# A planned attention-and-FFN kernel: new load sum, modelled instruction fetches, tanh in pairs and a split every fourth unit

## The chip, the cores and the metric

The kernel runs on one core of a Trainium2 chip. The metric is device time in microseconds; before the change it is 1190.25 us, the median of three runs from 1188.72 to 1191.48. Engines are written as in the profile: PE is TensorE, DVE is VectorE, ACT is ScalarE, POOL is GpSimd, SP is SyncE, whose queue issues all DMAs.

## The reference

For an input of 2048 tokens with 512 features the output is the sum of three things: the input, multi-head attention of its layer norm, and a gated FFN. Attention has 32 heads of only 16 features.

```
xn = _layernorm(x, axis=-1)
return x + _A_ref(xn, A_wqkv, A_wo) + _B_ref(xn, B_w1, B_w3, B_w2)
# _A_ref: q, k, v of xn @ wqkv, 32 heads of 16
scores = jnp.einsum("bhqd,bhkd->bhqk", q, k) * (Dh ** -0.5)
p = _softmax(scores, axis=-1)
o = jnp.einsum("bhqk,bhkd->bhqd", p, v)         # then o @ wo
# _B_ref: gate = x @ w1, up = x @ w3, F = 1792
h = _silu(gate) * up                            # then h @ w2
```

Scores for 32 heads, 2048 queries and 2048 keys are computed twice: once to find each query's maximum, once transposed for the exponentials.

## The kernel before

**Units.** Four heads share a tile of 128 partitions, 32 rows a head: 16 features, then two extra rows that carry the negative maximum in two parts of bf16, and rows that do not matter. A unit is four heads by 256 queries (128 at the start and in the last 16 units). There are 73 units, numbered 0 to 72.

**Pass 1, the maxima.** For each unit TensorE computes scores with queries on the partitions, two matmuls of 512 keys at a time (line 1164), and VectorE takes the maximum of these 1024 columns (line 1203). POOL joins the partial maxima, and a DMA transpose (line 1351) with two DMAs (line 1347) puts the negative maxima into the extra rows of the query tile QT.

**A split.** In some units, one of the 1024-column maxima is taken in part on ScalarE: TensorE forms a difference of two score blocks, ScalarE its relu (line 1271, into RB), and VectorE joins it with other scores in one combined instruction (line 1192). The dictionary SPLIT lists the units: from SPLIT_LO = 20 to 12 before the last, every SPLIT_STEP.

**Pass 2, the exponentials.** TensorE computes the scores transposed, keys on the partitions, with the maximum already subtracted, and ScalarE takes the exponential of a block of 512 columns (line 1477) or of two blocks in neighbouring PSUM banks (line 1507). A block is scored with 32 rows of the array by default (line 1452, "row"). It can also be scored over all 128 rows ("wide", lines 667 and 671, operand BD): BD holds a head's query rows with zeros in the other heads' rows, and four DMAs per unit, in bd_prep, copy 32 partitions each into it. PV (line 671, operand Vaug) multiplies the exponentials by the values and a column of ones; its result goes to U, is divided by way of small DMAs (Lc, rd, R) and lands in the tile for the output projection.

**The FFN** runs beside this in 56 chunks of 128 hidden features by 512 tokens. ffn_pair makes a gate tile (zg, line 966) and an up tile (ub, line 970); the tanh of zg (th, line 960) is put on lazyq, from which ScalarE takes work when it has a gap; POOL then makes t, a and hT with three instructions. zg, th and ub have two buffers, chosen by the chunk's parity.

**The order is planned.** The program builds one instruction list for each engine with a simulated clock. At each step every engine offers its next piece of work with an estimated start (pick_dve, pick_act, pick_pe, pick_pool, pick_sp), and the earliest is emitted. P.op, P.pe and P.dma estimate when an instruction starts and when its result can be seen. What has been emitted gets semaphore waits afterwards, in emit_engine; on the chip every engine runs its list in this order. Rules such as leads and limits are in RULES; for every 24 steps of the two passes TUNE names one entry of SETS that overrides some of them.

**The load sum.** _heat gives each TensorE instruction a weight, and heat(st) is the weighted sum over the last 2 us (RECENT). Under HEAT_FILL = 1.5 the planner may place a spare matmul (fill_cand: the identity times xnT, its result is never read). Under HEAT_WIDE = 0.9 it scores a block wide; under HEAT_P1 = 1.2 it may issue a pass-1 pair more than once; FFN tiles are held back above HEAT_TILE.

Of the kernel before, what the change touches and what calls it, by code (L numbers as in the profile page):

```python
# [7 lines left out]
ACTF = mybir.ActivationFunctionType  # L8
# [20 lines left out]
class _Item:  # L29
    __slots__ = ("fn", "reads", "writes", "occ", "lat", "cb", "pred", "name", "exp", "busy")  # L30

    def __init__(self, fn, reads, writes, occ, lat=None, cb=None, pred=None, name="", exp=None, busy=0.1):
        self.busy = busy
        self.fn = fn
# [10 lines left out]
class _Prog:  # L45
# [3 lines left out]
    def __init__(self):  # L49
# [12 lines left out]
        self.act_end = 0.0  # L62

# [82 lines left out]
    def pe(self, fn, reads, writes, mode, groups, dur, name="", first=None):  # L146
# [32 lines left out]
    def dma(self, fn, reads=(), writes=(), name="", eng="sp", lat=2.3, occ=0.62, busy=0.1):  # L179
# [11 lines left out]
        op.vis = start + lat + over  # L191
        self.ndma += 1
# [66 lines left out]
def _c_mm(n):  # L259
    return n / 2400.0 + (0.007 if n >= 512 else 0.004)  # L260
# [6 lines left out]
def _build(nc, A_x, A_wqkv, A_wo, B_w1, B_w3, B_w2, out):  # L267
# [28 lines left out]
    AUG_LAT = 3.0  # L296
# [25 lines left out]
    SPLIT_STEP = 5  # L322
# [7 lines left out]
        dict(ROW_LEAD=0.55),  # L330
# [3 lines left out]
        dict(A_LEAD=0.69),  # L334
        dict(TOL=0.05),
        dict(TOL=0.15),
        dict(PAIR_WAIT=0.1),
        dict(PV_LEFT=2),
        dict(RELAX=0.05),
# [3 lines left out]
        dict(HEAT_FILL=1.15),  # L343
        dict(HEAT_FILL=2.0),
        dict(HEAT_FILL=3.0),
        dict(HEAT_WIDE=1.15),
        dict(HEAT_WIDE=1.4),
        dict(HEAT_P1=1.5),
        dict(HEAT_TILE=1.3),
        dict(HEAT_TILE=1.6),  # L350
        dict(PAIR_WAIT=0.1, HEAT_FILL=2.0),
        dict(ROW_LEAD=0.55, WIDE_LEAD=0.45, BD_NEAR=0.1),
        dict(BD_NEAR=0.5, MIN_PIECE=2, TOL=0.15, HEAT_FORCE=1.0),
        dict(PV_LEFT=8, HEAT_WIDE=1.4, TOL=0.05, LAZY_GAP=0.02),
        dict(ROW_LEAD=0.4, TOL=0.05, MATE=0.0, HEAT_WIDE=0.0),
        dict(TEN_MID=2, PAIR_TEN=2, TOL=0.05),
        dict(MIN_PIECE=2, MATE=0.0, ROW_LEAD=0.5),
        dict(A_LEAD=0.6, HEAT_FORCE=1.0, WIDE_LEAD=0.7),
        dict(HEAT_FORCE=1.0, PAIR_WAIT=0.1, ROW_LEAD=0.43),
# [1765 lines left out]
```

## Time and profile before

| what | value |
| --- | --- |
| median of 3 runs | 1190.25 us |
| the profiled execution's own time | 1188.72 us |
| its span | 1187.0 us |
| granted TensorE clock, mean | 0.999 |
| PE busy | 1136.2 us, 96% |
| DVE busy | 1170.7 us, 99% |
| ACT busy | 1165.9 us, 98% |
| POOL busy | 459.4 us, 39% |
| DMA packets | 144068, 56.28 MB |

The span runs from the first to the last instruction; the execution's time is 1.7 us longer. A row of a group shows line, engine, operation, output and inputs, shapes and count, then busy time in us and mean ns of one, then the engine's idle time before it. A row of a timeline shows the start and the time from the first start to the last end in us, and how many equal instructions follow one another (x60). On VectorE and ScalarE an instruction starts before the one before it has ended, so the distance of two starts is the price of one, not its length. Idle times under 150 ns are not listed. Sums over groups hide this overlap; a wait is put down to the work that ended it.

### The profile page before, as it was taken

What the parts mean: (1) busy time and instruction counts of PE and PEld (TensorE: products, weight loads), DVE (VectorE), ACT (ScalarE), POOL (GpSimd) and SP (SyncE); (2) the same over time, 40 slices, a digit from 0 to 9 for tenths busy, and PEclk for the clock granted to TensorE, in tenths of its full rate; (3) what the DMA queues carried; (4) which work ended last, traced back from release to release, by engine and by line L of the source; (5) the groups of instructions that cost most, each with busy time, mean ns of one, the idle gap of its engine ahead of it and who ended that gap; (6) DMA issues with size and microseconds to landing.
All of it is one profiled execution on the core that took longest, in us unless ns stands there. A gap on an engine that the chain in (4) does not pass through costs nothing.

```text
span 1187.0 us, 35168 instructions
## 1 busy us (share of the span) xinstructions
PE 1136.2 (96%) x14555; PEld 518.3 (44%) x14555; DVE 1170.7 (99%) x1083; ACT 1165.9 (98%) x2216; POOL 459.4 (39%) x921
## 2 busy tenths in 40 slices
PE   8999999999999999999999999999999999999998
PEld 4443444433444444443444434443434443445554
DVE  8999999999999999999999999999999999999996
ACT  8899999999999999999999999999999999999998
POOL 6245454333423236344332245434332246233320
PEclk9999999999999999999999999999999999999999
DMA  7223231211111122111111122111110121111110
GB/s 244 65 61 97 73 89 41 61 27 42 38 29 40 37 62 49 36 42 31 40 33 27 40 67 50 32 41 33 39 34 23 40 67 23 28 26 23 22 21 22
DMA packets 144068, 56.28 MB, mean 47 GB/s; under 512 B 106028, under 2 KB 143908, under 8 KB 143908
## 3 DMA queue, kind: packets, MB, share of 16 engines
q1 hardware_dynamic: 143908, 54.02, 18.0%
q8 instruction: 115, 1.88, 0.7%
q14 instruction: 45, 0.37, 0.1%
HBM read 38.67 MB, written 6.74 MB: 38 GB/s over the span
## 4 chain that ended last, share of the span: by engine, by line
ACT 49%; PE 25%; DVE 21%; DMA 2%; issue 1%; POOL 1%; SPq 0%; ACTq 0%; POOLq 0%
ACT PT L1477 34%; DVE part L1203 21%; PE ps L667 10%; ACT PT L1507 9%; PE ps L671 5%; PE ps L1452 5%; PE ps L1164 4%; ACT zg L966 1%; ACT ub L970 1%; ACT th L960 1%; ACT U L1571 1%; PE ps L1813 1%; DMA rd<-Rc 1%; DMA BD<-QT 1%; ACT kq L855 1%
## 5 line engine op out<-in xcount | busy, mean ns | idle before, releaser
L1203 DVE TENSOR_REDUCE part<-ps 128x2 f32<-128x1024 f32 x1008 | 1143.1, 1216 | 2.5 <-PE ps L1452 1.6
L1477 ACT ACTIVATE PT<-ps 128x512 bf16<-128x512 f32 x1642 | 881.4, 691 | 4.6 <-PE ps L1452 1.8
L1452 PE MATMUL ps<-QT,KT 32*128 32x256 bf16 (+1 forms) x3520 | 456.3, 257 | 7.1 <-DMA QT<-Zs 0.4
L1164 PE MATMUL ps<-KT,QT 32*128 32x512 bf16 x2074 | 420.6, 383 | 5.4 <-DVE part L1203 2.9
L1452 PEld LDWEIGHTS ps<-QT,KT 32*128 32x128 bf16 x3520 | 162.4, 92 | 160.6 <-ACT PT L1477 72.2
L1507 ACT ACTIVATE PT<-ps 128x1024 bf16<-128x1024 f32 x203 | 219.9, 1117 | 0.0
L671 PE MATMUL ps<-PT,Vaug 128*17 128x256 bf16 (+1 forms) x4672 | 191.9, 261 | 4.7 <-ACT PT L1507 2.4
L1596 POOL TENSOR_TENSOR Rc<-Lc,mone 128x8 f32<-128x8 f32 (+1 forms) x69 | 105.0, 1522 | 225.1 <-DMA Lc<-U 224.8
L1164 PEld LDWEIGHTS ps<-KT,QT 32*128 32x128 bf16 x2074 | 104.2, 91 | 157.9 <-DVE part L1203 79.0
L667 PE MATMUL ps<-xnT,w 128*128 128x512 bf16 (+3 forms) x639 | 159.6, 320 | 5.3 <-ACT PT L1507 1.0
L667 PE MATMUL ps<-BD,KT 128*128 128x256 bf16 (+1 forms) x786 | 136.6, 266 | 5.4 <-ACT PT L1507 2.8
L671 PEld LDWEIGHTS ps<-PT,Vaug 128*17 128x17 bf16 x4672 | 89.7, 90 | 79.2 <-issue 52.9
L667 PE MATMUL ps<-xnT,ident 128*128 128x512 bf16 (+3 forms) x309 | 89.2, 335 | 12.3 <-DVE part L1203 4.5
L667 PEld LDWEIGHTS ps<-xnT,w 128*128 128x128 bf16 x639 | 49.8, 97 | 78.2 <-issue 39.0
L1328 POOL TENSOR_TENSOR mx<-part 128x16 f32<-128x16 f32 (+1 forms) x67 | 14.2, 212 | 180.2 <-DVE part L1203 180.0
L667 PEld LDWEIGHTS ps<-BD,KT 128*128 128x128 bf16 x786 | 62.3, 98 | 42.5 <-ACT PT L1477 9.5
L667 PE MATMUL ps<-w,hT 128*128 128x512 bf16 (+3 forms) x342 | 77.7, 309 | 0.0
L945 POOL TENSOR_SCALAR t<-th 128x512 f32<-128x512 bf16 x56 | 34.8, 622 | 104.8 <-ACT th L960 104.0
L949 POOL TENSOR_TENSOR hT<-a,t 128x512 bf16<-128x512 f32 x56 | 71.0, 1268 | 2.8
L671 PE MATMUL ps<-BD,KT 128*32 128x256 bf16 (+1 forms) x1464 | 68.4, 268 | 0.3 <-DMA BD<-QT 0.2
L947 POOL TENSOR_TENSOR a<-zg,ub 128x512 f32<-128x512 bf16 x56 | 64.6, 1154 | 9.5 <-ACT ub L970 9.5
L1616 POOL TENSOR_TENSOR wk_on<-U,R 128x256 bf16<-128x256 f32 (+1 forms) x36 | 23.0, 638 | 72.4 <-DMA R<-rd 72.4
(110 smaller groups left out, 710.4 us busy)
## 6 DMA issues: line engine op xcount, KB each, us to landing
w<-in_B_w_dram SPq DMA_DIRECT2D x112, 128.0 KB
R<-rd SPq DMA_DIRECT2D x55, 128.0 KB
QT<-qd SPq DMA_DIRECT2D x31, 128.0 KB
KT<-kd SPq DMA_DIRECT2D x28, 128.0 KB
BD<-QT SPq DMA_DIRECT2D x220, 16.0 KB
xr<-in_A_x_dram SPq DMA_DIRECT2D x16, 128.0 KB
out_dram<-osb SPq DMA_DIRECT2D x16, 128.0 KB
qd<-kq SPq DMA_DIRECT2D x15, 128.0 KB
```

Source lines behind the costliest of these rows:

```text
L667: return e.matmul(bank(bk)[:, c0 + a:c0 + b], make_lhsT(0, 128), rhs_ap(0)[:, a:b], start=start, stop=stop, **kw)
L671: ins = e.matmul(bank(bk)[32 * i:32 * i + m, c0 + a:c0 + b], make_lhsT(i), rhs if (a, b) == (0, ncols) else rhs[:, a:b], start=start, stop ...
L945: q.append(_Item(lambda e: e.tensor_scalar(t1[:, :], th[:, ss, :], 1.0, 1.0, ALU.mult, ALU.add), [("th", ss)], [("t1",)], 0.62, 0.72))
L947: q.append(_Item(lambda e: e.tensor_tensor(a32[:, :], zg[:, ss, :], ub[:, ss, :], ALU.mult), [("zg", ss), ("ub", ss)], [("a32",)], 1.1, 1.25))
L949: q.append(_Item(lambda e: e.tensor_tensor(hT[:, hslot(idx), :], a32[:, :], t1[:, :], ALU.mult), [("a32",), ("t1",)], [("hT", hslot(idx))] ...
L1164: ins = e.matmul(bank(2 * sl + i), QT[32 * j:32 * j + 32, qs, q * 128:(q + 1) * 128], KT[32 * j:32 * j + 32, g, c_ * 512:(c_ + 1) * 512], ...
L1203: redq.append(_Item(lambda e: e.tensor_reduce(dst, pair_ap.rearrange("p (a b) -> p a b", b=512), AX.X, ALU.max), writes, [("part", par, qt ...
L1452: ins = e.matmul(bank(b)[:, i * nq:(i + 1) * nq], KT[32 * j:32 * j + 32, g, (k0 + i) * 128:(k0 + i + 1) * 128], QT[32 * j:32 * j + 32, qs, ...
L1477: expq.append(_Item(lambda e: e.activation(PT[:, sl, :], bank(b), ACTF.Exp, scale=SCALE), [("ps", b)], [("PT", sl)], _c_act(512), cb=cb, e ...
L1507: return _Item(lambda e: e.activation(PT[:, s0:s1 + 1:s1 - s0, :], ps8[:, b0:b1 + 1:b1 - b0, :], ACTF.Exp, scale=SCALE), [("ps", b0), ("ps ...
L1596: poolq["nrm"].append(_Item(lambda e: e.tensor_tensor(Rc[:, pp, 0:nl], Lc[:, pp, 0:nl], mone[:, 0:nl], ALU.pow), [("Lc", pp), ("mone",)], ...
L1616: poolq["nrm"].append(_Item(lambda e: e.tensor_tensor(onorm[ob][:, g, q0:q0 + nq], U[:, us, 0:nq], R[:, pp, 0:nq], ALU.mult), [("U", us)] ...
```

## The change

Some of it alters what is emitted:

- Tanh is taken for two chunks together: one instruction of 128x1024 after the second chunk's gate, for chunks of even and odd number. POOL's work for the first chunk can start only then.
- SPLIT_STEP goes from 5 to 4.
- The copies into BD carry 21 partitions for 32. The rows that are left out stay zero from the start; the 16 features and the two extra rows are among the 21.

The rest alters the planner's estimates and rules, and so the order:

- _heat has new weights for every kind of matmul (the limits in RULES stay).
- P.pe counts TensorE's instructions and notes when it is expected to fetch the next 256 (_FETCH); P.dma makes a transfer that is not marked narrow land later if it coincides with a fetch.
- Expected latencies of several small transfers are lowered (AUG_LAT 3.0 to 2.55; the two extra rows 2.0 to 1.75; BD 2.1 to 2.0; R 3.7 to 3.5).
- SETS and TUNE are replaced.

```diff
+_FETCH = (180, 256, 2.0255, 25.5, 1.0, 2.05, 0.7, 0.15)
 def _heat(name, mode, groups, full, dur):
     if mode == "row":
-        return (0.846 if name.startswith("p2") else 0.713) * len(groups)
-    n = 1 if full else 8 if name.startswith("w2") else 4
-    return (1.23 if name.startswith("PV") else 2.32) + 0.0284 * n / dur
+        return (1.04 if name.startswith("p2") else 0.447) * len(groups)
+    if name.startswith("PV"):
+        return 2.16
+    if not full:
+        return 3.6
+    return 3.0 if name.startswith("w2") else 2.75
...
+        self.pe_n += _FETCH[2] * (mm or getattr(fn, "mm", 1))
+        if self.pe_n >= self.fetch_at:
+            self.fetch.append(start + _FETCH[4])
+            self.fetch_at += _FETCH[1]
...
+        if not narrow and self.heat:
+            soon = self.heat[-1][0] + (self.fetch_at - self.pe_n) / _FETCH[3] + _FETCH[4]
+            for t in self.fetch[-2:] + [soon]:
+                if start + _FETCH[6] - _FETCH[5] / 2 < t < op.vis - _FETCH[7]:
+                    op.vis = max(op.vis, t + _FETCH[5])
...
-    AUG_LAT = 3.0
+    AUG_LAT = 2.55
...
-    SPLIT_STEP = 5
+    SPLIT_STEP = 4
...
+            pair_done[idx] = part_done
+
             def zg_done(op):
-                lazyq.append(_Item(lambda e: e.activation(th[:, ss, :], zg[:, ss, :], ACTF.Tanh),
-                                   [("zg", ss)], [("th", ss)], 0.52, cb=part_done))
-                lazy_t[0] = P.free["act"]
+                if ss == 1:
+                    lazyq.append(_Item(lambda e: e.activation(th[:, :, :], zg[:, :, :], ACTF.Tanh),
+                                       [("zg", 0), ("zg", 1)], [("th", 0), ("th", 1)], 0.947,
+                                       cb=lambda op: [pair_done[i](op) for i in (idx - 1, idx)]))
+                    lazy_t[0] = P.free["act"]
                 part_done(op)
...
-                later_dma(lambda e, j=j: e.dma_start(BD[32 * j:32 * j + 32, u % 2, j, 0:nq],
-                                                     QT[32 * j:32 * j + 32, qs, q0:q0 + nq]),
+                later_dma(lambda e, j=j: e.dma_start(BD[32 * j:32 * j + 21, u % 2, j, 0:nq],
+                                                     QT[32 * j:32 * j + 21, qs, q0:q0 + nq]),
```

SETS goes from 55 to 52 entries, and TUNE's 128 numbers all refer to the new list.

More of the change, by code (lines that the diff above doesn't have):

```diff
@@ L144, in pe_start, with pe @@
         return t
-    def pe(self, fn, reads, writes, mode, groups, dur, name="", first=None):
+    def pe(self, fn, reads, writes, mode, groups, dur, name="", first=None, mm=0):
         op = _Op()
@@ L675, in part @@
                 f.full = full
+                f.mm = 1 if full else n
                 return f
@@ L1167, in f @@
                     return ins
-                P.pe(f, reads, writes, "row", rows, again * _c_mm(512) * (3 - len(rows)), name="p1_%d" % n, first="dve")
+                P.pe(f, reads, writes, "row", rows, again * _c_mm(512) * (3 - len(rows)), name="p1_%d" % n, first="dve",
+                     mm=again * len(cells))
                 p1_n[0] += 1
```

101 lines of the change are left out of this document (53 added, 48 removed), and 12 rows, old and new, of the table TUNE.

## The prediction

> **What bounds the kernel now.** I read the head of the page first, then the stages, then VectorE's and ScalarE's instructions in order of time, and last the chain.
>
> ```profile
> PE 1136.2 (96%) x14555; PEld 518.3 (44%) x14555; DVE 1170.7 (99%) x1083; ACT 1165.9 (98%) x2216; POOL 459.4 (39%) x921
> ACT 49%; PE 25%; DVE 21%; DMA 2%; issue 1%; POOL 1%; SPq 0%; ACTq 0%; POOLq 0%
> 58.00:1029.00 971.00, 937.26 (x11211) 407.97 (x11210) 970.80 (x866) 968.19 (x1838) 387.81 (x725) 1.00 0.18 45
> 1029.00:1168.00 139.00, 132.32 (x2523) 74.86 (x2522) 136.79 (x124) 136.01 (x264) 43.17 (x132) 1.00 0.10 21
> 1168.00:1187.00 19.00, 13.21 (x366) 7.83 (x362) 8.65 (x26) 13.97 (x19) 0.00 (x0) 0.95 0.09 30
> ```
>
> In the stage rows the columns are the stage, its length, then busy time of PE, weight loads, DVE, ACT and POOL, the granted clock, and the DMA share. Through the body VectorE (970.80 of 971) and ScalarE (968.19) are both full, so the page does not say which one sets the end. Busy time also hides waits shorter than an instruction's own latency, so I go by the distance from one start to the next.
>
> ```profile
> 13.90 1.23 DVE L1203 TENSOR_REDUCE part<-ps 128x2 f32<-128x1024 f32 x1
> 451.56 1.23 DVE L1192 CUSTOM_DVE_ANT_0 RB<-ps,RB 128x1024 f32<-128x1024 f32 x1
> 452.71 67.97 DVE L1203 TENSOR_REDUCE part<-ps 128x2 f32<-128x1024 f32 x60
> 1168.22 0.17 DVE L1357 TENSOR_REDUCE negm<-part 128x4 f32<-128x16 f32 x1
> 1169.39 0.29 DVE L916 TENSOR_SCALAR QT<-ps 128x128 bf16<-128x128 f32 x1
> ```
>
> VectorE's reduces step by (67.97 - 1.23) / 59 = 1.131 us where nothing holds them up. From the first reduce at 13.90 to the last maximum at 1168.22 there are 1154.3 us, and 1008 x 1.131 + 8 x 1.15 = 1149.2: only some 5 us of VectorE's main run are waits. So VectorE is saturated, but is it what ends last? The tail on ScalarE answers:
>
> ```profile
> 1170.16 0.62 ACT L1477 ACTIVATE PT<-ps 128x512 bf16<-128x512 f32 x1
> 1170.64 4.72 ACT L1507 ACTIVATE PT<-ps 128x1024 bf16<-128x1024 f32 x5
> 1175.16 1.18 ACT L1477 ACTIVATE PT<-ps 128x512 bf16<-128x512 f32 x2
> 1176.12 1.14 ACT L1507 ACTIVATE PT<-ps 128x1024 bf16<-128x1024 f32 x1
> 1177.02 0.73 ACT L1477 ACTIVATE PT<-ps 128x512 bf16<-128x512 f32 x1
> 1177.50 1.17 ACT L1507 ACTIVATE PT<-ps 128x1024 bf16<-128x1024 f32 x1
> 1178.40 0.75 ACT L1477 ACTIVATE PT<-ps 128x512 bf16<-128x512 f32 x1
> 1178.88 1.19 ACT L1507 ACTIVATE PT<-ps 128x1024 bf16<-128x1024 f32 x1
> 1179.78 1.27 ACT L1477 ACTIVATE PT<-ps 128x512 bf16<-128x512 f32 x2
> 1180.74 1.23 ACT L1507 ACTIVATE PT<-ps 128x1024 bf16<-128x1024 f32 x1
> ```
>
> The last unit's query rows are ready at 1169.68. From 1170.16 on ScalarE still does 25 blocks of exponentials of 512 columns (a row of 1024 is two). The last unit, with 128 queries, has 16 of them. Nine are left over from units whose maxima were ready long before, and at 0.48 us (below) these are 4.3 us. So the end is set by ScalarE, which is behind its feed, and VectorE has about 4.3 us to spare. After the last exponential at 1181.97 come PV, the division, the last output tile and the store, 5.0 us that the change leaves alone.
>
> **The change part by part.** The sums are against the profiled execution, span 1187.0 and time 1188.72 us; the median of the runs is 1190.25, 1.5 above, and I add my difference to that.
>
> ScalarE's prices, start to start:
>
> ```profile
> 444.20 0.65 ACT L1271 ACTIVATE RB<-ps 128x512 f32<-128x512 f32 x1
> 444.68 0.66 ACT L1477 ACTIVATE PT<-ps 128x512 bf16<-128x512 f32 x1
> 445.16 0.67 ACT L1271 ACTIVATE RB<-ps 128x512 f32<-128x512 f32 x1
> 459.25 1.12 ACT L1507 ACTIVATE PT<-ps 128x1024 bf16<-128x1024 f32 x1
> 460.15 0.72 ACT L960 ACTIVATE th<-zg 128x512 bf16<-128x512 bf16 x1
> 460.67 0.69 ACT L1477 ACTIVATE PT<-ps 128x512 bf16<-128x512 f32 x1
> ```
>
> *Tanh in pairs.* 56 tanh of 512 columns at 0.52 become 28 of 1024. No row has a tanh of 1024; an exponential of 1024 takes 0.90 against 0.48 for 512, so 512 more columns cost 0.42, and I take 0.52 + 0.42 = 0.94. The saving is 28 x (1.04 - 0.94) = 2.8 us. Bounds: 0 (a pair as dear as two) and 28 x (1.04 - 0.90) = 3.9. What it delays: POOL's products of the first chunk of a pair wait for the second chunk's gate. POOL is busy 39%, and nobody is near needing these products except the next pair's own start, so I cost this at nothing; without that cover a late product would hold back filler matmuls, not scores.
>
> *Splits every fourth unit.* Units are numbered 0 to 72. Every fifth from 20 gives nine, of which unit 60 has no second half, so eight; every fourth gives eleven, again without unit 60, so ten. One split replaces four reduces by two reduces and one combined instruction (1.15, from 451.56 to 452.71): VectorE saves 2 x 1.131 - 1.15 = 1.11, for two splits 2.2 us. ScalarE gets four more relu at 0.48 (444.20 to 444.68): +1.9 us, or 4 x 0.45 = 1.8 where they go in pairs. TensorE and POOL get a few instructions each, which lie beside other work. So the splits move work from the engine with 4.3 us to spare to the one that ends last.
>
> *Copies of 21 rows and the instruction fetches.* The fetch bookkeeping issues nothing; it makes the planner's landing times later for wide transfers. The masked copies keep their count and queue and carry 21 rows for 32.
>
> ```profile
> q8 instruction: 115, 1.88, 0.7%
> BD<-QT SPq DMA_DIRECT2D x220, 16.0 KB
> PE ps L667 <- DMA BD<-QT: 0.8, 1, 0.8
> PE ps L1452 <- DMA QT<-Zs: 0.4, 1, 0.4
> PE ps L671 <- DMA BD<-QT: 0.2, 1, 0.2
> ```
>
> All waits of TensorE for these transfers come to 1.4 us. That is all that better landing times can win, and the engine that ends last feels them only in part: I take -0.5, bounds -1.4 and +1.4 (the smaller latencies could just as well make such waits). The Trainium skill (DMA: Bandwidth & Descriptors, "Why a DMA increments its semaphore by 16 and not by 1") says that a transfer uses the largest number of engines up to 16 that divides its outer size: 16 for 32 rows, 7 for 21. By that the copies miss the engines above, where a fetch may sit, and this term would be -1.0, the two waits for BD gone; no run so far shows which engines they use.
>
> *The load sum.* The planner adds a spare matmul, or scores a block over the whole array, when its weighted sum of TensorE's work over 2 us is under a limit. The limits stay; the weights change.
>
> ```profile
> L1452 PE MATMUL ps<-QT,KT 32*128 32x256 bf16 (+1 forms) x3520 | 456.3, 257 | 7.1 <-DMA QT<-Zs 0.4
> L1164 PE MATMUL ps<-KT,QT 32*128 32x512 bf16 x2074 | 420.6, 383 | 5.4 <-DVE part L1203 2.9
> L667 PE MATMUL ps<-xnT,ident 128*128 128x512 bf16 (+3 forms) x309 | 89.2, 335 | 12.3 <-DVE part L1203 4.5
> ```
>
> At one column per 1/2400 us, 2074 matmuls of 512 columns are 442 us of work in their row groups: 0.713 to 0.447 takes 118 from the sum over the run. 3520 of 256 (some 128) are at most 375 us: 0.846 to 1.04 adds up to 73. The other projections, wide scores and spare matmuls rise by 0.15 to 0.75 a us. With all groups I get a sum 4% higher for the old order, so a little fewer spare matmuls: a tenth of 309 at about 0.16 us, 5 us of TensorE in 1136. A gain from that would show as fewer small waits of ScalarE. How large these are:
>
> ```profile
> 1134.65 8.71 ACT L1477 ACTIVATE PT<-ps 128x512 bf16<-128x512 f32 x17
> 1143.24 0.28 ACT L920 ACTIVATE QT<-ps 128x128 bf16<-128x128 f32 x1
> ```
>
> Here an exponential takes (1143.24 - 1134.65) / 17 = 0.505 against 0.48 undisturbed: 0.025 us of waiting each, over 1642 of them up to 41 us for the run. A new order, with every rule of its 128 segments dealt anew, redistributes these. I take 0 for it, with bounds of a tenth of 41 us for the better and, since a list that fits badly has no floor, a quarter for the worse: -4 and +10.
>
> Sum on ScalarE: -2.8 + 1.9 - 0.5 + 0 = -1.4 us. VectorE's -2.2 is not added, it lengthens a slack. Span 1187.0 - 1.4 = 1185.6, median 1190.25 - 1.4 = 1188.85.
>
> **Rivals.**
> - *Both engines gain.* The new order uses the freed VectorE time and ScalarE arrives at the last unit without the nine leftover blocks. For it: VectorE would then have to set the end, and it does so 2.2 earlier; the leftover is 4.3. Together at most -6.5 (1183.7), and half of the leftover gives -4.4 (1185.9). Against: ScalarE must find this in its small waits, and it got 1.9 us of relu on top.
> - *The order fits worse, slower.* Place: score matmuls that wait in TensorE's queue behind spare and projection matmuls. Price: a tenth more of the 41 us is +4.1 - 1.4 = +2.7 (1193.0), a quarter is +8.9 (1199). It decides the sign from 1.4 us on, and is outside "no change" from 3.8. For it: VectorE has only 5 us of waits in 1154 now, which leaves more to lose than to win. Against: TensorE's own waits for DMA are small.
> - *The clock drops.* The granted clock is 1.00 in every stage up to 1168, and 0.95 in the last. Fewer spare matmuls could let it fall in between. In the last stage 5% of 19 us are lost, 1 us; with TensorE busy 132 of 139 us, each us lost in the body delays scores by nearly as much. Three falls like that would be +3 - 1.4 = +1.6 (1191.9), ten +8.6 (1198.9). Against: at the new weights the sum is only 4% off the old one, and the limits hold it from below. The Trainium skill (TensorE: Matmul & The Clock Gate, "The HAM clock gate") has the clock halve after an idle window of some 3.4 us; no stage before 1168 shows it.
> - *Nothing changes:* the 41 us and the ends fall out as before and the two ScalarE terms cancel: 1190.25.
>
> **How the numbers follow.** Two tenths of a per cent, 2.4 us, is about what a measurement can tell here. The forecast with the "nothing" rival holds 0.37: times from 1187.9 to 1192.6. Both engines gain: 0.33. A worse order: 0.22. Clock: 0.08. So faster 0.33, same 0.37, slower 0.30. The forecast's own range is 1187 to 1190.5. Cases of both signs are likely, so the whole range reaches from 1184.5 (-5.75, short of the -6.5) to 1196 (+5.75, somewhat over half of the way to the quarter).
>
> **What would show it.** Tanh: 28 instructions of 128x1024, each followed by the next start after about 0.94. Splits: ten combined instructions, 1004 reduces stepping by 1.131, last maximum near 1166.0. ScalarE as the end: more than nine leftover blocks after the last maximum, or a last exponential near 1180.6. Copies: no wait of TensorE for BD. Load sum: about 280 spare matmuls, the clock at 1.00 up to the tail. The prediction is wrong if the leftover is gone (first rival), if VectorE's waits exceed 8 us (second), or if a stage before the tail has less than 1.00 (third).

## The result

The changed kernel takes 1194.92 us, the median of 22 runs (1190.93 to 1201.85); beside it the kernel before takes 1191.05 (1188.52 to 1198.96, 22 runs). The ratio is 1.0027, with a 95% interval from 1.0014 to 1.0040: slower by some 3 us, outside what a measurement can mistake for no change. The forecast was no change, 1188.85, in a range up to 1196. The profiled execution took 1196.14 us with a span of 1194.4, 1.2 above its median, where that of before was 2.3 below (1188.72 against 1191.05). So the two traces differ by 7.4 us, the medians by 3.9. Two runs, one of the kernel before (1236.9 us) and one of r_oldheat (1222.5), count as slow, with a far lower clock than the others of their kernel, and are left out throughout.

The stages of the changed kernel, in the columns of the prediction's stage rows:

```profile
58.00:1029.00 971.00, 908.98 (x10991) 406.55 (x11097) 969.27 (x867) 966.55 (x1803) 382.19 (x723) 1.00 0.18 44
1029.00:1168.00 139.00, 125.54 (x2533) 74.09 (x2549) 131.53 (x119) 130.24 (x256) 46.66 (x135) 0.98 0.09 19
1168.00:1194.00 26.00, 20.75 (x483) 11.98 (x486) 14.92 (x31) 21.38 (x37) 1.92 (x3) 0.96 0.09 27
```

Up to 1029 us VectorE and ScalarE are as full as before. The loss lies in the next stage: VectorE is busy 131.53 us of 139 where it was 136.79, ScalarE 130.24 where it was 136.01, and the granted clock is 0.98 where it was 1.00. Both engines lose alike, which points to what feeds both, TensorE. The groups, and the waits of TensorE for a transfer and of VectorE for TensorE (total, times, longest):

```profile
PE 1107.5 (93%) x14448; PEld 518.7 (43%) x14586; DVE 1169.6 (98%) x1083; ACT 1165.0 (98%) x2187; POOL 459.1 (38%) x925
L1229 DVE TENSOR_REDUCE part<-ps 128x2 f32<-128x1024 f32 x1004 | 1139.8, 1210 | 9.3 <-PE ps L1478 5.2
L1478 PE MATMUL ps<-QT,KT 32*128 32x256 bf16 (+1 forms) x3592 | 467.9, 258 | 20.1 <-DMA QT<-Zs 6.4
L684 PE MATMUL ps<-xnT,ident 128*128 128x512 bf16 (+3 forms) x260 | 74.1, 329 | 9.9 <-ACT PT L1534 2.3
```

```profile
PE ps L1478 <- DMA QT<-Zs: 6.4, 5, 2.3
DVE part L1229 <- PE ps L1478: 5.2, 5, 2.4
DVE part L1229 <- PE ps L1189: 3.0, 5, 1.2
```

In the first of these rows 138 matmuls lack a record (14448 for 14586 weight loads), where the trace of before has all, so the busy time of PE (1107.5 us for 1136.2) can't be compared.

TensorE, which waited 0.4 us for the rows of QT before, now waits 6.4 us. In VectorE's timeline, 5.0 of the 8.2 us in its two rows follow a wait of TensorE for QT, 0.7 a wait for BD (1.1 us on TensorE), and 2.6 lie around a fall of the clock, from 1076 to 1083. The distances of starts on VectorE:

```profile
14.55 1.23 DVE L1229 TENSOR_REDUCE part<-ps 128x2 f32<-128x1024 f32 x1
434.08 1.20 DVE L1218 CUSTOM_DVE_ANT_0 RB<-ps,RB 128x1024 f32<-128x1024 f32 x1
435.22 35.25 DVE L1229 TENSOR_REDUCE part<-ps 128x2 f32<-128x1024 f32 x31
1174.68 0.17 DVE L1383 TENSOR_REDUCE negm<-part 128x4 f32<-128x16 f32 x1
```

From the first reduce to the last maximum there are 1160.1 us, and the work in them is 1004 x 1.131 + 10 x 1.14 = 1146.9. So 13.2 us are waits, where the prediction found some 5. With the later start (0.65) that is the whole story of this trace: 2.3 us of work gone, 8.1 us of waits come, and a last maximum 6.5 us later (1174.68 for 1168.22).

How such a wait comes about stands in the timeline, here late in the run. SP's queue of DMAs:

```profile
1130.80 1.13 SPq L1377 DMA_TRANSPOSE Zs<-Z  x1
1131.97 0.61 SPq L1632 DMA_DIRECT2D R<-rd  x1
1132.63 0.56 SPq L1619 DMA_DIRECT2D Lc<-U  x1
1136.23 1.07 SPq L1373 DMA_DIRECT2D QT<-Zs  x2
```

And TensorE beside it:

```profile
1135.87 0.33 PE L1478 MATMUL ps<-QT,KT 32*128 32x128 bf16 x3
1138.48 0.38 PE L1478 MATMUL ps<-QT,KT 32*128 32x128 bf16 x4 [2.28 <-DMA QT<-Zs]
```

VectorE stands behind it:

```profile
1139.91 5.98 DVE L1229 TENSOR_REDUCE part<-ps 128x2 f32<-128x1024 f32 x5 [2.42 <-PE ps L1478]
```

The two rows can be sent only when the transpose has landed: from 1130.80 to 1136.23 it took 5.4 us, where the planner reckons 2.55 in this kernel and reckoned 3.0 before. TensorE's next score matmul waits 2.28 us, and no other work is put in front of it. In the records of the DMA queues a fetch of TensorE's instructions (queue q8: 115 of 16 KB, one for about 256 of its instructions) starts meanwhile, at 1134.10. But by then, 3.3 us after its issue, a usual transpose has landed, and a load of 128 KB (xr) that was issued 0.5 us ahead of it is late too (4.1 us, where such a load takes 2.3 in the middle). So what held this transpose up is not shown. Over the trace, the 16 transposes that meet a fetch take 2.3 to 5.6 us, 3.8 in the middle, and all six of over 4 us are among them; the 51 others take 2.4 in the middle and 3.7 at most. In the trace of before four took 4.0 to 4.9 us as well, and TensorE waited 0.4 us: there the order had room for them.

The clock is the other part. Four stretches around the fall:

```profile
1072.20:1075.60 3.40, 2.69 (x73) 1.71 (x71) 2.96 (x3) 2.73 (x6) 0.00 (x0) 1.00 0.16 17
1075.60:1079.00 3.40, 2.81 (x29) 1.65 (x31) 2.50 (x3) 3.02 (x6) 2.22 (x7) 0.50 0.05 9
1079.00:1082.40 3.40, 3.40 (x57) 2.14 (x55) 2.37 (x2) 2.44 (x5) 0.78 (x4) 0.50 0.05 7
1082.40:1085.80 3.40, 3.39 (x115) 2.28 (x112) 3.22 (x3) 3.20 (x8) 0.00 (x0) 0.99 0.25 57
```

After 3.4 us in which TensorE was busy 2.69, the clock is halved for two stretches of 3.4 us. VectorE does 2.50 + 2.37 us of work in these 6.8 us: 1.9 us lost, about 1 us a stretch. Up to the fall TensorE stood still for 0.83 us, for which the profile shows no cause (its row says issue).

Over the runs the clock says more than one trace. The mean granted clock was 0.9935 for the changed kernel and 0.9977 for the kernel before (the first 37 runs beside the experiments below; over 122 of them it is 0.9975). Among the 22 runs of the changed kernel, a straight line of time against lost clock has a slope of 0.69 us per thousandth (correlation 0.71). Between the means of these two sets of runs, 1195.4 and 1190.1, there are 5.3 us; 4.1 thousandths of clock are 2.9 of them, and 2.4 are left. (The ratio, which compares runs on one chip, is 3.2 us.) This division is an estimate. A hole in TensorE's work costs time by itself and can bring a fall, so the line may put too much on the clock. The 122 runs of the kernel before have a like slope, 0.75, but the ten of after_shift below have 0.13. And one more run of the kernel before has a recorded clock of 0.949 and took 1189.44 us; no trace of it is left, and it stays unexplained.

### The profile page after: what moved, and what is told of

It is laid out like the page before. It is cut to its first block, busy times and chain, and to the rows that moved or that the text cites. A ratio compares the mean times of both kernels' runs of the same rounds, so it can differ in the third digit from the quotient of the medians.

```text
span 1194.4 us, 35070 instructions
## 1 busy us (share of the span) xinstructions
PE 1107.5 (93%) x14448; PEld 518.7 (43%) x14586; DVE 1169.6 (98%) x1083; ACT 1165.0 (98%) x2187; POOL 459.1 (38%) x925
## 4 chain that ended last, share of the span: by engine, by line
ACT 58%; PE 19%; DVE 14%; DMA 4%; issue 3%; POOL 2%; SPq 1%; ACTq 0%; POOLq 0%
ACT PT L1504 41%; DVE part L1229 14%; ACT PT L1534 9%; PE ps L684 7%; PE ps L1478 5%; PE ps L688 4%; PE ps L1189 3%; ACT zg L991 2%; ACT th L984 2%; ACT ub L995 1%; ACT U L1598 1%; DMA Zs<-Z 1%; ACT kq L874 1%; DMA QT<-Zs 1%; ACT RB L1297 1%
## 5 line engine op out<-in xcount | busy, mean ns | idle before, releaser
L1478 PE MATMUL ps<-QT,KT 32*128 32x256 bf16 (+1 forms) x3592 | 467.9, 258 | 20.1 <-DMA QT<-Zs 6.4
L1189 PE MATMUL ps<-KT,QT 32*128 32x512 bf16 x2090 | 426.7, 384 | 13.2 <-DVE part L1229 6.7
L1478 PEld LDWEIGHTS ps<-QT,KT 32*128 32x128 bf16 x3592 | 169.2, 93 | 179.5 <-ACT PT L1504 74.5
L1534 ACT ACTIVATE PT<-ps 128x1024 bf16<-128x1024 f32 x208 | 226.8, 1129 | 0.5 <-PE ps L1478 0.2
L684 PE MATMUL ps<-xnT,w 128*128 128x512 bf16 (+3 forms) x603 | 148.6, 311 | 13.2 <-ACT U L1598 3.8
L684 PE MATMUL ps<-BD,KT 128*128 128x256 bf16 (+1 forms) x718 | 127.2, 268 | 8.0 <-ACT PT L1534 6.1
L684 PE MATMUL ps<-xnT,ident 128*128 128x512 bf16 (+3 forms) x260 | 74.1, 329 | 9.9 <-ACT PT L1534 2.3
L688 PE MATMUL ps<-BD,KT 128*32 128x256 bf16 (+1 forms) x1448 | 62.9, 261 | 1.1 <-DMA BD<-QT 1.1
L1643 POOL TENSOR_TENSOR on_b<-U,R 128x256 bf16<-128x256 f32 (+1 forms) x33 | 23.4, 709 | 94.2 <-DMA R<-rd 94.2
```

The costliest lines, as they stand in the source:

```text
L684: return e.matmul(bank(bk)[:, c0 + a:c0 + b], make_lhsT(0, 128), rhs_ap(0)[:, a:b], start=start, stop=stop, **kw)
L688: ins = e.matmul(bank(bk)[32 * i:32 * i + m, c0 + a:c0 + b], make_lhsT(i), rhs if (a, b) == (0, ncols) else rhs[:, a:b], start=start, stop ...
L1189: ins = e.matmul(bank(2 * sl + i), QT[32 * j:32 * j + 32, qs, q * 128:(q + 1) * 128], KT[32 * j:32 * j + 32, g, c_ * 512:(c_ + 1) * 512], ...
L1478: ins = e.matmul(bank(b)[:, i * nq:(i + 1) * nq], KT[32 * j:32 * j + 32, g, (k0 + i) * 128:(k0 + i + 1) * 128], QT[32 * j:32 * j + 32, qs, ...
L1534: return _Item(lambda e: e.activation(PT[:, s0:s1 + 1:s1 - s0, :], ps8[:, b0:b1 + 1:b1 - b0, :], ACTF.Exp, scale=SCALE), [("ps", b0), ("ps ...
L1643: poolq["nrm"].append(_Item(lambda e: e.tensor_tensor(onorm[ob][:, g, q0:q0 + nq], U[:, us, 0:nq], R[:, pp, 0:nq], ALU.mult), [("U", us)] ...
```

## The experiments

In all kernels below nothing is left out of the computation. Ratios are to the kernel before, run beside each on the same chip. "Clock lost" is one minus the mean granted clock, averaged over the runs, in thousandths. The last column is worked out from the trace of the profiled execution: for every TensorE instruction the weight that the old load sum gives it, over its streaming time, averaged over the last 3.41 us; the share of the run, from 25 to 1170 us, where this is under 1.1. It is an estimate: all traces but that of before lack the records of some 140 matmuls, most of them over the whole array. With these put in from their weight loads, a share can come out at twice or half of what stands here, or for the small ones still further off, by what is taken as a matmul's streaming time. Either way r_same, r_oldheat, after and after_bd32 have several times the share of the kernel before.

| kernel | median us | ratio, 95% interval | clock lost | load under 1.1 |
| --- | --- | --- | --- | --- |
| before | 1189.9 to 1191.1 | 1 | 2.3 | 0.45% |
| after | 1194.92 | 1.0027 [1.0014, 1.0040] | 6.5 | 1.39% |
| before_bd21 | 1192.85 | 1.0025 [1.0009, 1.0042] | 4.8 | 0.34% |
| before_shift | 1189.70 | 1.0004 [0.9981, 1.0027] | 3.2 | 0.18% |
| after_bd32 | 1197.22 | 1.0057 [1.0036, 1.0079] | 7.2 | 0.83% |
| after_shift | 1193.78 | 1.0032 [1.0022, 1.0043] | 5.4 | 0.47% |
| after_spare2 | 1217.89 | 1.0229 [1.0210, 1.0248] | 2.8 | |
| r_same | 1208.12 | 1.0150 [1.0119, 1.0180] | 25.5 | 2.45% |
| r_oldheat | 1204.52 | 1.0124 [1.0105, 1.0143] | 24.8 | 1.62% |
| r_same_c | 1191.57 | 1.0010 [0.9995, 1.0025] | 3.0 | 0.59% |
| r_oldheat_c | 1187.72 | 0.9979 [0.9965, 0.9993] | 2.1 | 0.68% |
| r_oldheat_c_again | 1189.10 | 0.9997 [0.9979, 1.0015] | 3.4 | |
| r_oldheat_c_shift | 1190.23 | 0.9996 [0.9981, 1.0012] | 2.8 | |
| r_oldheat_mar_c | 1192.23 | 1.0015 [1.0000, 1.0029] | 2.3 | 0.43% |
| r_same_k2 | 1189.66 | 0.9986 [0.9968, 1.0004] | 1.5 | 0.27% |
| r_oldheat_k2 | 1191.83 | 1.0004 [0.9985, 1.0024] | 3.2 | 0.37% |
| r_same_floor | 1226.51 | 1.0287 [1.0253, 1.0320] | 4.5 | |
| after_floor | 1206.34 | 1.0140 [1.0106, 1.0173] | 2.2 | |

### The order kept: twice the spare matmuls

```diff
+                def twice(e):
+                    g(e)
+                    return g(e)
-                P.pe(col_groups(bk, ...
+                P.pe(twice,
```

> The changed order, but each spare matmul is issued twice in its place; nothing else moves in the lists. Clock theory (the new load sum places too little work, TensorE's clock falls in the body): the mean granted clock rises from 0.987-0.998 to 0.998-0.999 in all runs and the time falls by about 3 us to 1191-1192, though TensorE has some 50 us more to do. Late-maxima theory (the transposed maxima land later than the tighter plan assumes): the clock may rise, but the time stays at 1195 or goes up by what the extra matmuls delay, and the waits of TensorE for the QT rows stay at about 6 us.

The clock came back to a mean of 0.997, but the time rose by 23 us to 1217.89. The waits of VectorE for TensorE show part of why:

```profile
DVE part L1229 <- PE ps L1478: 13.5, 36, 1.9
DVE part L1229 <- PE ps L1189: 3.9, 12, 0.5
```

TensorE's order leaves little room for spare work put in blindly: 48 waits where there were ten, 17.4 us for 8.2. The rest of the 23 us is not in these rows, which leave out waits under 0.15 us. Here more load held the clock and cost more than the clock gave.

### The copies undone, and the copies alone

```diff
# after_bd32
-                later_dma(lambda e, j=j: e.dma_start(BD[32 * j:32 * j + 21, u % 2, j, 0:nq],
+                later_dma(lambda e, j=j: e.dma_start(BD[32 * j:32 * j + 32, u % 2, j, 0:nq],
# before_bd21: the same lines of the kernel before, 32 to 21
```

> The changed order, but the masked copies carry 32 rows again. If the 21-row copies keep clear of TensorE's instruction fetches, the copies get slower near a fetch, TensorE waits for BD about 1 to 2 us more and the time rises by 0 to 2 us, to 1195-1197. If they do not matter, 1195 within 1 us. Late-maxima theory: the waits for the QT rows come at the same places as in the changed kernel's trace (near 920, 941, 1115, 1125 and 1136 us), 4 to 8 us in all. Clock theory: falls of the clock, at other places than 1075, with a mean clock of 0.99-0.998.

> The order before, only the masked copies carry 21 rows. If the copies' width matters, TensorE's waits for BD (1.0 us) go away and the time falls by 0 to 1 us, to 1190-1191; packets fall by about 5500. If it does not, 1191 as before. The clock stays at 0.999 by the clock theory, as the order is the one before.

Neither agrees with a simple price. With 32 rows in the changed order the time is 1.0057 (TensorE waits 4.2 us for BD, four times), so there the narrow copies seem worth some 3.5 us (the intervals of the two ratios just touch). With 21 rows in the order of before it is 1.0025, slower, with 1.3 us of waits for BD and 0.5 for QT; two of its 12 runs had a clock of 0.985 and 0.986 and took 1199.1 and 1197.7. The kernel before has such runs too (0.985 to 0.988 in five of 122), so it may be chance; otherwise, why a transfer that is early should cost an order clock is open.

after_bd32 shows one thing more. It has the order and the fetches of the changed kernel, and its trace was expected to have the late rows of QT at the same places, 4 to 8 us in all. It has one:

```profile
PE ps L1478 <- DMA QT<-Zs: 1.1, 1, 1.1
```

It stands at 923 us, where the changed kernel has one; those at 1117, 1126 and 1138 us are gone. So most of the 6.4 us are of one execution.

What the narrow copies do to the DMA engines is plain. The queue of all data transfers, before and after:

```profile
q1 hardware_dynamic: 143908, 54.02, 18.0%
```

```profile
q1 hardware_dynamic: 138388, 52.62, 17.3%
```

There are 5520 packets fewer, 276 copies (four for each of 69 units) with 20 fewer each; 11 of the 20 are rows, and nine are left over, which fits completions of 7 engines in place of 16. The rule of the Trainium skill that the prediction cited (DMA: Bandwidth & Descriptors, "Why a DMA increments its semaphore by 16 and not by 1") gives just these nine, with 16 engines becoming 7.

### The fetches moved against the work

```diff
-        P.op("pe", lambda e: e.matmul(bank(4)[:, 0:1], ...
+        def first_mm(e):
+            for _ in range(128):
+                e.nop(nofuse=True)
+            return e.matmul(bank(4)[:, 0:1], ...
+        P.op("pe", first_mm,
```

> The order of the changed kernel, with 128 empty instructions ahead of TensorE's first matmul, so that all later fetches of TensorE's instructions fall half a block earlier against the work. Nothing else differs. Late maxima (a transpose that meets a fetch comes 2 to 3 us late and stalls TensorE): the waits for QT near 919, 1115, 1125 and 1136 us (6.4 us in the sum over the kernel) vanish or move to other places; where they vanish the time falls by 2 to 3 us, to 1192 to 1193; where others of that size take their place it stays at 1195, but the places differ. Clock theory: the load is the same, so the granted clock stays at 0.990 to 0.996 and the time at 1194 to 1196, and the waits for QT do not matter.

> The kernel before, order unchanged, with 128 empty instructions ahead of TensorE's first matmul, so that its fetches fall half a block earlier against the work. If the order of before owes part of its time to where its own fetches happen to fall (its AUG_LAT of 3.0 leaves the transposes 0.45 us more than the changed kernel's 2.55), the time rises by 1 to 3 us, to 1191 to 1193, with waits for QT or BD of 2 us or more and a clock under 0.998 in more runs. If its latencies cover any fetch, it stays within 1 us of 1190.2 and its clock at 0.998.

In the profile of after_shift, the fastest of its runs, the waits for QT are down to a sixth.

```profile
PE ps L1482 <- DMA QT<-Zs: 1.0, 2, 0.9
```

As they are 1.1 us in after_bd32 too, where no fetch was moved, this does not show that the fetches had made them. The ratio did not fall in any case: 1.0032 against 1.0027, and the clock lost is 5.4 against 6.5. So in the median the late rows of QT are not what makes the changed kernel slow; the theory that put its loss on them alone fell here. The order of before does not mind where its fetches fall: 1.0004.

Late transfers may have a part in the clock, though. The traces of after, after_bd32 and after_shift, which share one order, have five falls before 1170 us. Three of them come 0.1 to 1.3 us after TensorE had waited over 1 us for BD: 1.54 us up to 944.53 (fall at 945.8), 1.25 up to 1095.92 (1096.0), 1.19 up to 1090.19 (1090.6). The lower latencies alone are not the cause: r_same_c and r_same_k2 below plan with them too and lose 3.0 and 1.5 thousandths.

### A new order, with the newer and with the old load sum

```diff
# r_same: only TUNE
-    TUNE = (11, 32, 8, 0, 14, 2, 3, 28, 19, 36, ...
+    TUNE = (42, 32, 1, 19, 41, 33, 14, 47, 43, 16, ...
# r_oldheat: _heat of before as well, and TUNE
+    TUNE = (42, 51, 40, 12, 44, 50, 9, 42, 51, 43, ...
```

With any planner rule altered, the 128 numbers of TUNE deal another order, so a part of the planner can only be undone together with a new choice of TUNE. It was chosen by one greedy pass: at each segment every entry of SETS is tried, followed for three more segments, and the one kept after which the planner has both engines done earliest.

> The changed kernel's rules with TUNE chosen anew, by one greedy pass over the 128 segments: another order from the same load sum and the same latencies. The plan has less load than the changed kernel's (mean 1.60 against 1.64, 2.4% of its stretches of 3.4 us under 1.1 against none). Clock theory: the clock loses as much as in the changed kernel or more (mean 0.993 or lower), time 1194 to 1199. Late maxima: waits for QT of 3 to 8 us in the sum again, as the latencies are the same, time 1192 to 1196 whatever the clock.

> As the kernel with TUNE chosen anew (same greedy pass), but with the load sum's weights of the kernel before. If the newer load sum itself is the cause, this one is 2 us or more faster than that one and its clock is higher by 0.003 or more. If the load sum is no cause, both agree within 2 us and differ only by where their waits for QT fall. Its plan has 2.2% of stretches of 3.4 us under 1.1, so by the clock theory in its general form (lowest load counts, not the weights) both lose clock alike: 0.990 to 0.995.

Both are far slower, 1208.12 and 1204.52. The gap between them is over the 2 us that the expectation had named, but their intervals overlap, and the clock is not higher with the old sum (24.8 and 25.5 lost). The stages of r_same:

```profile
58.00:400.00 342.00, 319.65 (x3856) 137.46 (x3889) 332.40 (x294) 332.03 (x620) 132.28 (x244) 0.96 0.20 51
400.00:700.00 300.00, 282.11 (x3259) 122.10 (x3290) 290.70 (x260) 290.26 (x548) 114.21 (x216) 0.95 0.15 37
700.00:1029.00 329.00, 309.74 (x3592) 131.77 (x3629) 326.67 (x294) 326.39 (x608) 126.44 (x247) 0.99 0.16 40
```

The clock is lost in every stage, and VectorE's time with it: 9.6 us of 342 in the first. TensorE's waits for transfers are small (1.1 us for QT and 3.8 for BD over the whole run), so most of this is the clock. It was dearer than either theory had it, and it comes with both sets of weights.

### The same, with a price on low load

To the planner's score in the greedy pass is added a penalty for how far the load, averaged over 3.4 us, falls short of 1.25. Only TUNE differs from r_same and r_oldheat (the planner then places 409 spare and 457 wide score matmuls for r_same's 298 and 412).

> As the kernel with TUNE chosen anew with the newer load sum, but the greedy pass also penalised stretches of 3.4 us with a load under 1.25: more spare and wide matmuls (409 and 457 against 298 and 412 planned), lowest stretch 1.03, no stretch in ten thousand under 1.1. Clock theory: the clock comes back to 0.998 or 0.999 and the time to 1188 to 1191. Late maxima: the latencies are unchanged, so waits for QT of 3 to 8 us, and 1193 to 1197 in spite of the clock.

> As the newly chosen order with the penalty on stretches of low load (1191.57 with the newer load sum), but with the load sum of the kernel before, both for the planner's limits and for the penalty. Its plan has 0.2% of its stretches under 1.1, like that one's. If the weights of the newer sum are no worse and no better a measure of what holds the clock, it agrees with that one within 1.5 us (1190 to 1193, clock 0.996 to 0.999). If the newer sum is the cause of the lost clock, it is 2 us or more faster (under 1189.5) with a clock of 0.999 in most runs.

All or nearly all that the two orders before had lost is back: 1191.57 and 1187.72. The first stages of r_same_c:

```profile
58.00:400.00 342.00, 322.26 (x3960) 142.50 (x3999) 341.14 (x303) 339.10 (x638) 135.88 (x253) 1.00 0.20 52
400.00:700.00 300.00, 285.04 (x3347) 127.80 (x3382) 299.63 (x269) 299.08 (x569) 115.88 (x220) 1.00 0.16 40
```

The 3.9 us between the two would convict the newer load sum; the expectation had drawn that line at 2. So the pair was drawn again, with a pass that looks two segments ahead:

> A second draw of an order with the newer load sum and the penalty on stretches of low load (the greedy pass looks two segments ahead, not three). The two pairs so far, same search with the newer and with the old sum, gave 1.0150 against 1.0124 and 1.0010 against 0.9979 of the kernel before. If the newer sum itself costs 2 to 4 us, this one comes out at 1190 to 1192.5, 2 us or more behind its pair. If these differences are the luck of single orders, it lies within 1.5 us of its pair, or ahead of it. Its plan has no stretch under 1.1, so its clock should hold 0.998 or more in the mean.

> The pair of it with the load sum of the kernel before, same search. If the old sum is better in itself: 1187 to 1189, ahead of the kernel before, 2 us or more ahead of its pair. If the order decides: anywhere from 1187 to 1192, within 1.5 us of its pair or behind it. No stretch of its plan is under 1.1 by its own weights, so its clock should hold 0.998 or more in the mean.

Now the newer sum is 2.2 us ahead, 1189.66 against 1191.83. Three pairs, two for the old sum and one for the new: single orders differ by 2 to 4 us with the sign changing, so no such gap convicts either sum, and a smaller effect of the sum is not excluded. The best of them was run again, as it is and with its fetches moved:

> The same kernel once more, in another call. If 0.9979 was not the luck of one chip and one call: 0.997 to 0.999 again, 1187 to 1189. If it was picked from noise: 0.999 to 1.001.

> The order that was 0.9979 of the kernel before, with 128 empty instructions ahead of TensorE's first matmul, so that all fetches meet the work elsewhere. If that order owed its place to where fetches fall, this goes back to 1190 to 1192, with waits for QT or BD of 2 us or more; if not, it stays at 1187 to 1189.

0.9997 and 0.9996, where it had 0.9979: its lead is not confirmed, and no version was shown to beat the kernel before. As the intervals overlap, a lead of 1 us or so is not excluded either. The shifted one took 1190.23, in the range that was to mean that the order owed its place to its fetches, and its trace has a wait of 2.8 us for BD beside a fall of the clock; but the unshifted one had lost its lead alike.

### More room for the small transfers

```diff
-    AUG_LAT = 2.55
+    AUG_LAT = 3.8
-  ... "QTr%d" % r), lat=1.75, narrow=True,
+  ... "QTr%d" % r), lat=2.3, narrow=True,
-  ... [("rd", pp)], RK, lat=3.5, busy=1.4, narrow=True, cb=n5)
+  ... [("rd", pp)], RK, lat=3.9, busy=1.4, narrow=True, cb=n5)
```

This goes with the old load sum, the price on low load and its own TUNE.

> As the one before with the load sum of before and the penalty, and with more room for the small transfers: transposes planned at 3.8 us for 2.55, the two extra rows at 2.3 for 1.75, R at 3.9 for 3.5. Late maxima: the waits for QT are 0 to 0.5 us in the sum, no hole of TensorE of over 1 us is left from them, and the clock holds 0.999; the plan is 1.6 us longer than that one's, so 1190 to 1191.5, no gain in the median but a narrower spread (under 4 us from lowest to highest). If late maxima were no cause of the holes, the clock and the spread stay as in that one and the time is 1.5 us above it.

TensorE's waits for QT are gone from its profile, as expected, and the clock lost is 2.3. But it takes 1192.23 and ranges from 1188.68 to 1196.46, where a spread of under 4 us and 1190 to 1191.5 were expected. In this one order, room for the transfers is no gain once the load is held.

### The order kept: spare matmuls only where the load was low

```diff
+        more = _EXTRA.get(len(self.ops["pe"]), 0)
+        if more:
+            inner = fn
+            def fn(e, inner=inner, more=more, bk=writes[0][1]):
+                for _ in range(more):
+                    self.spare(e, bk)
+                return inner(e)
...
+        P.spare = lambda e, bk: e.matmul(bank(bk)[:, 0:512], ident[:, 0:128], xnT[:, 0, 0:512], start=True, stop=True)
```

> The newly chosen order that lost most clock (1208.12 us, clock 0.967), unchanged, with 220 spare matmuls of 512 columns issued ahead of 181 of its score pieces, into the bank that the piece itself then overwrites; they are put where the load over 3.41 us, worked out from its trace, was under 1.15, at pieces whose reader came late by 1.1 us on average. Load theory: the clock rises to 0.992 or more and the time falls by 10 us or more, to 1190 to 1198. If the order is the cause and the clock a companion: the spare matmuls only cost TensorE time (220 at 0.213 us, 47 us in queues with little to spare), and the time stays at 1208 or rises.

> The changed kernel's order, unchanged, with 112 such spare matmuls ahead of 95 pieces, where the load of its own traces was under 1.1. Load theory: mean clock from 0.9935 to 0.997 or more; the 3 us of time that go with it come back, less what the matmuls cost (by the 355 that cost 23 us, 0.065 us each, 7 us where there is no slack; the pieces are chosen by slack, so 0 to 4 us): 1191 to 1196. If the clock stays under 0.995 with the load lifted, the load sum misses what makes it fall here.

The clock did what the load theory says: with the order unchanged, the loss of r_same went from 25.5 to 4.5 thousandths, that of the changed kernel from 6.5 to 2.2. So load, not some other feature of these two orders, holds the clock. The trace of after_floor still has waits for transfers, 3.9 us for BD and 1.1 for QT, and no fall before its end: with load around them, such holes did not bring one. The times went the other way, to 1226.51 and 1206.34. Two stages of r_same_floor, and its waits:

```profile
58.00:400.00 342.00, 325.90 (x3889) 138.40 (x3930) 332.35 (x293) 332.74 (x618) 132.22 (x244) 1.00 0.20 51
400.00:700.00 300.00, 287.10 (x3356) 125.42 (x3388) 294.17 (x262) 294.10 (x551) 114.22 (x217) 1.00 0.15 38
```

```profile
DVE part L1246 <- PE ps L1206: 22.6, 48, 1.7
DVE part L1246 <- PE ps L1495: 7.7, 18, 0.9
```

At a clock of 1.00 VectorE loses in the first stage what it lost at 0.96 (332.35 against 332.40), now waiting for score matmuls behind the added ones. At full clock r_same_floor takes 1221 us (two of its runs); r_same, by a line through its six runs (0.77 us per thousandth, correlation 0.95), would take 1188. The difference over 220 added matmuls is 0.15 us for each, and for after_floor (1205.5 - 1190.9) / 112 = 0.13. A spare matmul that stands behind a bank's wait, just ahead of the score that is awaited, costs 60 to 70% of the 0.216 us at which matmuls of its shape follow one another in the trace of before. I had chosen the places by the slack of the reader alone, and not by what else was queued on TensorE.

## Why the prediction was wrong

**The step that failed** is the term for the new order, "I take 0 for it", and in it the third rival, "The clock drops", with its chance of 0.08 and the reason against it: "the sum is only 4% off the old one, and the limits hold it from below". A limit on a planned average over 2 us did not hold the lowest stretches on the chip. (On the trace of before, instruction by instruction, the new weights give a sum only 1.4% higher, not 4%; the reason was no better for it.) In place of 0 the order cost 5.3 us between the means, with some 2.9 of them going with the clock. The rival's price was right, in part by luck, for it was taken from the last stage, where the clock falls after the last exponential. The prediction had "three falls like that" at +3 us. The changed kernel's mean clock is 4.1 thousandths lower than that of before; half rate loses half of its time, so this is 2 x 0.0041 x 1194 = 10 us more at half rate, three stretches of 3.4 us, and the line through its runs prices them at 2.9 us. Whether the low stretches behind them were in the order itself, or came of late transfers that it left no room for, is not separated. That "no stage before 1168 shows it" was true of the one execution I had. Over its runs the kernel before loses 2.3 thousandths, so it has falls as well, and a stage of several hundred us rounds one of them away.

**"What would show it"** named two marks of failure, and both came: a stage before the tail under 1.00 (0.98), and waits of VectorE over 8 us (13.2). The second was meant for scores stuck behind spare matmuls. It came from late rows of QT and from the clock instead. A third sign failed too: TensorE's waits for BD, forecast to go, are 1.6 us (1.0 before). One reading held: ScalarE still ends last, with ten blocks left over from earlier units where there were nine.

**The landing times.** "All waits of TensorE for these transfers come to 1.4 us. That is all that better landing times can win" was right as a gain; the bound on the loss, +1.4, was not a bound. In the profiled execution the waits for QT grew to 6.4 us. A wait of 0.4 us in the old trace showed that the planned 3.0 us were enough in that order, not that 2.55 would be. But this execution is not the median: in after_bd32 and after_shift most of these waits are gone and the ratio is no lower, so I do not count them as shown in the 3 us.

**The terms of the sum.** Tanh: 28 instructions, and the pair costs what was worked out, 0.94 us from one start to the next.

```profile
471.93 0.83 ACT L1504 ACTIVATE PT<-ps 128x512 bf16<-128x512 f32 x1
472.41 1.29 ACT L984 ACTIVATE th<-zg 128x1024 bf16<-128x1024 bf16 x1
473.35 0.83 ACT L995 ACTIVATE ub<-ps 128x512 bf16<-128x512 f32 x1
```

Splits: 1004 reduces and ten combined instructions, as said. Spare matmuls: 295 by their weight loads (260 have a record), 14 fewer than before, where "about 280" was said. The -1.4 of the sum can't be read off a trace: the last exponential of unit 49 comes at 920.2 for 921.7, but from unit 20 to unit 52 this lead goes from 2.6 us to -0.3 and back, and by the end the changed kernel is 7.4 us behind. At equal clock (the lines carried to no loss) the changed kernel stands at 1190.9 and the kernel before at 1188.4, and the five orders with a price on low load (the repeats aside) lie from 1185.6 to 1190.4, 1188.3 in the mean, no better than before. (The lowest, r_oldheat_c, comes out at 1186.5 and 1187.2 in its repeats.) Whether the greedy orders waste these 1.4 us, or saved work on two engines that are both full only shows if TensorE keeps up, the runs do not settle. The 2.5 us by which the changed kernel is behind at equal clock stay open as well; late transfers are argued for them, not shown.

**The bounds of that 0** had the same fault. Orders from the same rules differed by 17 us (r_same and r_same_c). For an order that is dealt anew the bound of +10 for the worse, from small waits of ScalarE, had the wrong quantity behind it.

## What to carry to other kernels

When a change deals TensorE's work anew, look at the lowest stretches of a few us and not at the mean: orders with a mean load of 1.60 to 1.62 (1.63 before, worked out as for the table) lost anything from next to nothing to some 20 us by their low end. One trace shows one draw of the clock's falls, so take the granted clock of every run and fit the time against it. Keep fillers out of the way of awaited work: those put ahead of awaited scores held the clock and cost two to five times what it gave (33 us for 16, 14.6 for 3.0).

## What the runs showed of the hardware

**The clock goes by fixed stretches.** In each trace all changes of the granted clock lie on one grid of 3.413 us, whose phase differs from run to run: in r_same the falls at 166.6, 231.4, 272.4, 303.1, 521.6, 613.7 and 763.9 us are 19, 12, 9, 64, 27 and 44 such steps apart. That is why falls move between runs of one kernel. Two of them, with the stretch before:

```profile
299.70:303.10 3.40, 2.56 (x25) 0.77 (x21) 3.40 (x4) 3.40 (x6) 2.37 (x5) 1.00 0.02 1
303.10:306.50 3.40, 2.95 (x19) 0.77 (x20) 2.61 (x4) 2.65 (x6) 0.00 (x0) 0.50 0.22 64
...
610.30:613.70 3.40, 2.62 (x26) 0.88 (x26) 3.40 (x4) 3.40 (x7) 0.00 (x0) 1.00 0.03 2
613.70:634.20 20.50, 19.50 (x184) 7.22 (x187) 14.45 (x12) 14.66 (x25) 4.07 (x10) 0.50 0.11 26
```

**It falls without idleness.** In the stretches ahead of these two falls TensorE was busy 75% of the time, by its records never idle for over 0.45 us at a time, and VectorE and ScalarE, which it feeds, were busy all of it. Over 15 traces, with the load worked out as for the table and averaged over each stretch of the grid in which the clock was full: under 1.0 the clock fell after 10 of 11 stretches, from 1.0 to 1.1 after 9 of 26, from 1.1 to 1.2 after 7 of 110, above that after 1 of 4819. With the newer sum's weights it is 10 of 15, 6 of 20, 8 of 89 and 3 of 4842. These counts are estimates like the last column of the table: with the missing matmuls put in and the columns alone as streaming time, the old weights give 10 of 16, 11 of 54, 3 of 164 and 1 of 4719. The steep rise of falls towards 1.0 stays, and which of the two sums is the better measure does not come out. Being busy is a far poorer one: over 18 traces, 55 stretches without a fall have a load (old weights) as low as nine in ten of those before a fall; by the share of time in which any columns stream there are 770. The Trainium skill (TensorE: Matmul & The Clock Gate, "The HAM clock gate") gives a window of about 3.4 us, and the traces agree with that length; it calls the window before a fall idle, and there these falls differ.

**A fall costs 0.7 to 1 us a step, and its length varies.** VectorE lost 1.9 us in two steps at half rate (above), and 6.0 in the six steps from 613.70, 20.5 us in which it did 14.45 us of work. The longest fall lasts eight steps: in r_oldheat, from 1072.5 to 1099.8, VectorE did 21.7 us of work in 27.3. Why some stay down is not shown.

**A transpose by DMA is often late when it meets a fetch.** In the trace of the changed kernel it takes 2.4 us in the middle without a fetch of TensorE's instructions meanwhile and 3.8 with one; the two longest were late before their fetch began. The copies into BD, with 21 rows for 32, went from a 90th percentile of 3.00 us, issue to landing, to 1.92, and in the order of before to 2.35.
